# New instruction lists and PSUM banks for an attention block with cached keys and values

## The chip, the cores and the metric

The kernel runs on one core of a Trainium2 chip. The metric is the device time of one execution in microseconds (us), as the median of several runs. A profile of one execution shows where its time goes.

## The reference

```python
B, Sq, D = 8, 112, 640
H, Sk, Dh = 32, 512, 192
def reference(x, k_cache, v_cache, wq, wo):
    q = (x @ wq).reshape(B, Sq, H, Dh).transpose(0, 2, 1, 3)
    scores = jnp.einsum("bhqd,bhkd->bhqk", q, k_cache) * (Dh ** -0.5)
    p = softmax(scores, axis=-1)
    o = jnp.einsum("bhqk,bhkd->bhqd", p, v_cache)
    return o.transpose(0, 2, 1, 3).reshape(B, Sq, H * Dh) @ wo
```

All inputs are bf16. There is no mask; the keys and values are as long for every query.

## The kernel before

The 32 heads are worked in four rounds of 8 heads, and a round goes through the 8 batches. One batch of one round has its 8 heads in two halves, so there are 64 *steps* n = 0 to 63, each with four heads. Two *groups* g of four batches share a round, g = 0 to 7.

The program is a set of named operations. Each has an engine, the operations that it depends on, and an `emit` function that issues its instructions:

- ('XT', c) transposes a piece of x on TensorE (PE), and ('evX', c) copies it from PSUM to SBUF.
- ('Q', g, lp, c) is five matmuls of 448 columns that make 128 rows of the queries of a group (line 720 of the profile), and ('evQ', g, lp, c) copies them to `qr` as bf16 (line 146 on ScalarE (ACT), line 147 on VectorE (DVE)). ('qc', n) copies halves of them to `qh` (lines 761 and 762).
- ('KN', i, ...) loads plain keys of the first seven batches, ('KT', i, p) transposes a pair of heads of them with 24 small matmuls (line 672), and ('evK', i, p, t) copies the halves to `kt`. The keys of later batches, ('K', i), are transposed by DMA as they are loaded.
- ('Sm', n, j) and ('St', n, j) are the scores of a step: four matmuls each, the first on the whole array, the second on two halves of its rows at once (line 773).
- ('smax', n, i) scales one head's scores out of PSUM and takes its extreme (DVE, line 830), ('exp', n, i) is the exponential (ACT, line 835), ('rc', n, j) the reciprocal of the sums (DVE, line 847), ('norm', n, i) the scaling of the probabilities (DVE, line 839).
- ('PT', n) transposes the probabilities with 32 small matmuls (line 874), and ('evPT', n, 0) and ('evPT', n, 1) copy the narrow (768 columns) and the wide part (1024) to `pT_sb`. For five late steps a DMA does it, ('TD', n).
- ('PVt', n) and ('PVm', n, j) multiply by the values, the first on halves of the array's columns (line 906), the second on the whole array (line 918); ('evPV', n) copies the result to `oT_sb` (ACT).
- ('O', g, m, part) multiplies by wo (line 940), ('oacc', g, m) adds up over rounds in `accT` (DVE). ('O6', ...), ('OL', ...) and ('oaccL', ...) are the same for the last two batches, ('OF', b) transposes the result back, ('oout', b) copies it out of PSUM, ('OUT', b) stores it.
- ('V', i, half), ('WQ', r, lp, n) and ('WO', r, half) are loads of values and weights.

An engine does its operations strictly in the order of a list that stands in the program as a table: `ORDER_PE`, `ORDER_ACT`, `ORDER_DVE` and `ORDER_SP` (the queue on SyncE that issues all DMAs). `BANKS` gives the PSUM bank of every result that PE makes. Waits follow from the dependencies, and two rules add more: whoever writes a bank waits until its previous contents were copied out, and a load waits until the load some 1.5 MB ahead of it in `ORDER_SP` has landed:

```python
AHEAD = 0.95
for i, op in enumerate(ORDER_SP):
    behind = [k for k in range(i) if sum(map(size, ORDER_SP[k + 1:i])) >= AHEAD]
    if behind and op[0] != "OUT":
        P.ops[op]["deps"] = P.ops[op]["deps"] + [ORDER_SP[behind[-1]]]
for op in ORDER_PE:
    for bank, evacs in tiles(op):
        P.ops[op]["banks"] = P.ops[op]["banks"] + holder.get(bank, [])
        holder[bank] = evacs
```

An operation's list also decides its engine. A copy out of PSUM runs on ACT or DVE, whichever list holds it:

```python
def copy(name, e, dst, src):
    if P.ops[name]["eng"] == "ACT":
        return e.activation(dst, src, ACTF.Copy)
    return e.tensor_copy(dst, src)
```

A load of keys or values reuses one of four or three buffers, so it also waits for the step that last read it; a load of wq waits for the Q matmuls of the round before.

Of the kernel before, what the change touches and what calls it, by code (L numbers as in the profile page):

```python
# [52 lines left out]
def build_mha_kernel(nc, x, k_cache, v_cache, wq, wo, out):  # L53
# [33 lines left out]
    with ExitStack() as es:  # L87
# [145 lines left out]
        def pv_all(n):  # L233
# [11 lines left out]
            ('PVm', 0, 0), ('PVm', 0, 1), ('PVt', 1), ('PVm', 1, 0), ('PVm', 1, 1), ('KT', 3, 3), ('Sm', 4, 0),  # L245
# [17 lines left out]
            ('Sm', 15, 0), ('Sm', 15, 1), ('St', 15, 0), ('St', 15, 1), ('PT', 13), ('PVt', 12), ('PVm', 12, 0),
            ('PVm', 12, 1), ('PVt', 13), ('PVm', 13, 0), ('PVm', 13, 1), ('Sm', 16, 0), ('Sm', 16, 1), ('St', 16, 0),
            ('St', 16, 1), ('PT', 14), ('Q', 3, 0, 1), ('Q', 3, 2, 0), ('Q', 3, 1, 0), ('Sm', 17, 0), ('Sm', 17, 1),
            ('St', 17, 0), ('St', 17, 1), ('PT', 15), ('PVt', 14), ('PVm', 14, 0), ('PVm', 14, 1), ('PVt', 15),
# [20 lines left out]
            ('Sm', 31, 1), ('St', 31, 0), ('St', 31, 1), ('PT', 29), ('O', 2, 4, 1), ('PVt', 28), ('PVt', 29),
            ('PVm', 29, 0), ('PVm', 29, 1), ('PVm', 28, 0), ('PVm', 28, 1), ('Sm', 32, 0), ('Sm', 32, 1), ('St', 32, 0),
            ('St', 32, 1), ('PT', 30), ('O', 2, 3, 0), ('Q', 5, 0, 0), ('O', 2, 3, 1), ('Q', 5, 2, 0), ('Sm', 33, 0),
            ('Sm', 33, 1), ('St', 33, 0), ('St', 33, 1), ('PT', 31), ('Q', 5, 3, 2), ('Q', 5, 1, 0), ('Sm', 34, 0),  # L290
            ('Sm', 34, 1), ('St', 34, 0), ('St', 34, 1), ('PVt', 30), ('PVt', 31), ('PVm', 30, 0), ('PVm', 30, 1),
# [910 lines left out]
```

## Time and profile before

| what | value |
|---|---|
| median of 3 runs | 439.31 us (437.9 to 439.82) |
| the profiled execution | 438.76 us, span of its instructions 437.0 us |
| PE busy | 423.3 us, 97% of the span |
| DVE busy | 363.1 us, 83% |
| ACT busy | 343.7 us, 79% |
| matmuls, weight loads | 6805 each |
| moved by DMA | 122.04 MB, 279 GB/s |

The span runs from the first to the last instruction; the run's time has 1.76 us around it. In the rows that follow, a line such as L720 is a line of the program, "x5" counts instructions, and a wait stands in brackets with what ended it; "issue" means that the profile shows nothing that the engine waited for.

### The profile page before, as it was taken

How to read it: one execution, taken by the hardware profiler on the slowest of the kernel's cores; microseconds unless marked ns; L12 is line 12 of the kernel's file. 1: busy time of each engine (PE TensorE's matmuls, PEld its weight loads, DVE VectorE, ACT ScalarE, POOL GpSimd, SP SyncE). 2: the span in 40 equal slices, each digit the busy share in tenths (PEclk: the TensorE clock that was granted, in tenths of full speed). 3: DMA queues.
4: the chain of work that ended last, by engine and by line, in shares of the span. 5: the costliest groups of instructions: out<-in, count | busy, mean ns of one | idle time of the engine just before them, and what ended most of it. 6: DMA issues, size and time to landing. Idle time of an engine off the chain costs nothing.

```text
span 437.0 us, 16234 instructions
## 1 busy us (share of the span) xinstructions
PE 423.3 (97%) x6805; PEld 290.2 (66%) x6805; DVE 363.1 (83%) x1169; ACT 343.7 (79%) x770; POOL 0.7 (0%) x6
## 2 busy tenths in 40 slices
PE   7999979999999999999999999999999999999996
PEld 4666756667677566666667666666766666576896
DVE  1479987989699889898999887889799878999872
ACT  2699979998579787988878777887878856985774
POOL 0000000000000000000000000000000000000000
PEclk9999999999999999999999999999999999999999
DMA  7998999999999999999999999999999999999972
GB/s 255 366 354 289 331 358 287 213 289 342 238 288 286 283 256 257 362 263 255 308 240 237 337 255 256 364 352 287 232 242 376 204 247 349 289 252 252 239 201 82
DMA packets 222858, 122.04 MB, mean 279 GB/s; under 512 B 165312, under 2 KB 222784, under 8 KB 222784
## 3 DMA queue, kind: packets, MB, share of 16 engines
q1 hardware_dynamic: 222784, 120.99, 106.6%
q8 instruction: 54, 0.88, 0.8%
q14 instruction: 20, 0.16, 0.1%
HBM read 78.22 MB, written 1.15 MB: 182 GB/s over the span
## 4 chain that ended last, share of the span: by engine, by line
PE 85%; DVE 7%; ACT 4%; DMA 2%; issue 1%; SPq 0%; DVEq 0%; ACTq 0%
PE ps L940 19%; PE ps L720 19%; PE ps L773 18%; PE ps L918 12%; PE ps L906 7%; PE ps L874 5%; DVE s_sb L830 4%; PE ps L672 2%; ACT p_sb L835 2%; DMA wq_sb<-in_wq_dram 2%; DVE p_sb L839 1%; ACT kt L146 1%; PE ps L973 1%; ACT qr L146 1%; DVE pT_sb L147 1%
## 5 line engine op out<-in xcount | busy, mean ns | idle before, releaser
L835 ACT ACTIVATE p_sb<-s_sb,nmx 112x512 bf16<-112x512 f32 x256 | 183.0, 718 | 32.8 <-DVE s_sb L830 25.6
L830 DVE TENSOR_SCALAR_CACHE_REDUCE s_sb<-ps 112x512 f32<-112x512 f32 x256 | 169.2, 683 | 23.3 <-PE ps L773 19.1
L720 PE MATMUL ps<-xT_sb,wq_sb 128*128 128x448 bf16 x480 | 103.2, 356 | 3.1 <-DMA wq_sb<-in_wq_dram 2.1
L773 PE MATMUL ps<-kt,qr 128*128 128x256 bf16 (+1 forms) x512 | 95.6, 273 | 1.1 <-ACT oT_sb L146 0.4
L940 PE MATMUL ps<-oT_sb,wo_sb 128*128 128x448 bf16 (+1 forms) x480 | 93.3, 341 | 0.3 <-DVE pT_sb L147 0.2
L773 PE MATMUL ps<-kt,qh 128*128 128x256 bf16 (+1 forms) x512 | 87.5, 272 | 0.0
L839 DVE TENSOR_SCALAR p_sb<-p_sb,rinv 112x512 bf16<-112x512 bf16 x256 | 81.2, 346 | 1.5
L720 PEld LDWEIGHTS ps<-xT_sb,wq_sb 128*128 128x128 bf16 x480 | 43.1, 98 | 41.9 <-DMA wq_sb<-in_wq_dram 2.8
L940 PEld LDWEIGHTS ps<-oT_sb,wo_sb 128*128 128x128 bf16 x480 | 44.3, 98 | 35.4 <-DVE pT_sb L147 0.8
L146 ACT ACTIVATE oT_sb<-ps 128x672 bf16<-128x672 f32 x64 | 46.1, 725 | 22.3 <-PE ps L918 21.7
L773 PEld LDWEIGHTS ps<-kt,qr 128*128 128x128 bf16 (+1 forms) x512 | 44.3, 96 | 25.7 <-issue 14.3
L146 ACT ACTIVATE qr<-ps 128x448 bf16<-128x448 f32 x96 | 49.7, 541 | 12.8 <-PE ps L720 12.1
L146 ACT ACTIVATE pT_sb<-ps 128x768 bf16<-128x768 bf16 x59 | 47.0, 800 | 10.3 <-PE ps L874 10.2
L918 PE MATMUL ps<-pT_sb,vt 128*128 128x112 bf16 x944 | 54.9, 213 | 0.0
L918 PEld LDWEIGHTS ps<-pT_sb,vt 128*128 128x128 bf16 x944 | 47.4, 98 | 4.1
L835 ACT ACTIVATION_READ_ACCUMULATOR p_sb<-s_sb,nmx 112x1 f32 x256 | 49.7, 194 | 0.0
L773 PEld LDWEIGHTS ps<-kt,qh 128*128 128x128 bf16 (+1 forms) x512 | 43.9, 96 | 6.1
L147 DVE COPY pT_sb<-ps 128x1024 bf16<-128x1024 bf16 x59 | 40.2, 682 | 2.4 <-PE ps L874 1.3
L874 PE MATMUL ps<-ident,p_sb 64*128 64x64 bf16 (+1 forms) x1888 | 37.4, 186 | 0.9 <-DVE p_sb L839 0.5
L874 PEld LDWEIGHTS ps<-ident,p_sb 64*128 64x128 bf16 (+1 forms) x1888 | 33.2, 94 | 6.9 <-DVE p_sb L839 2.6
L906 PE MATMUL ps<-pT_sb,vt 128*64 128x112 bf16 x944 | 32.8, 215 | 1.4 <-DVE s_sb L830 0.5
L906 PEld LDWEIGHTS ps<-pT_sb,vt 128*64 128x64 bf16 x944 | 25.5, 110 | 12.2 <-issue 3.4
(53 smaller groups left out, 228.2 us busy)
## 6 DMA issues: line engine op xcount, KB each, us to landing
vt<-in_v_cache_dram SPq DMA_DIRECT2D x64, 768.0 KB, 6.7
wo_sb<-in_wo_dram SPq DMA_DIRECT2D x8, 960.0 KB, 8.2
wq_sb<-in_wq_dram SPq DMA_DIRECT2D x14, 480.0 KB, 5.7
wo_sb<-in_k_cache_dram SPq DMA_DIRECT2D x6, 768.0 KB, 7.1
accT<-in_k_cache_dram SPq DMA_DIRECT2D x6, 768.0 KB, 7.2
vt<-in_k_cache_dram SPq DMA_DIRECT2D x2, 768.0 KB, 8.5
out_dram<-xT_sb SPq DMA_DIRECT2D x8, 140.0 KB, 2.5
wq_sb<-in_wq_dram SPq DMA_DIRECT2D x1, 960.0 KB, 7.5
```

What stands on the lines that cost most here:

```text
L146: return e.activation(dst, src, ACTF.Copy)
L147: return e.tensor_copy(dst, src)
L672: ends = [e.transpose(psb[:, bank + t, y * 64:(y + 1) * 64], kn[i][64 * t:64 * t + 64, 2 * p + u, c * 128:(c + 1) * 128], ident[64 * t:64 ...
L720: mm = e.matmul(ps[:, bank, 0:SG], w, v, start=(dc == 0), stop=(dc == DC - 1))
L773: return e.matmul(ps[:, 2 * j + odd, hs], q, ktb[j][lo:hi, :, blk, h * 128:(h + 1) * 128], start=first, stop=last, skip_group_check=True)
L830: return e.tensor_scalar(s_sb[:, a, :].rearrange("p (e c) -> p e c", e=2), ps[0:SQ, 2 * j:2 * j + 2, h * 256:(h + 1) * 256], -scale, None, ...
L835: return e.activation(p_sb[:, k, :], s_sb[:, a, :], ACTF.Exp, bias=nmx[:, k:k + 1], scale=-1.0, accum_out=rsum[:, k:k + 1])
L839: return e.tensor_scalar(p_sb[:, k, :], p_sb[:, k, :], rinv[:, k:k + 1], None, op0=ALU.mult)
L874: ends.append(e.transpose(psb[:, bank + t, i * w:(i + 1) * w], p_sb[lo:hi, (4 * n + k) % 8, q * 128:(q + 1) * 128], ident[lo:hi, lo:hi]))
L906: mm = e.matmul(ps[64 * h:64 * h + 64, b0 + j, SQ:2 * SQ], vtb[:, h0 + 2 * j + h, d0:d0 + 64], pT(j, h, q), start=(q == 0), stop=(q == 3))
L918: mm = e.matmul(ps[:, b0 + j, 2 * h * SQ:(2 * h + 1) * SQ], vtb[:, h0 + 2 * j + h, d0:d0 + 128], pT(j, h, q), start=(q == 0), stop=(q == 3))
L940: mm = e.matmul(ps[:, bank_of["O", g, m], 0:nc_], wo_sb[:, k, m * 128:(m + 1) * 128], oT_sb[:, g % 2, k, 0:nc_], start=(k == 0), stop=(k = ...
```

## The change

`ORDER_PE`, `ORDER_ACT`, `ORDER_DVE`, `ORDER_SP` and `BANKS` are replaced by others. The new tables were searched offline in two steps, first with a K or V load as one piece, and then with its halves as pieces of their own. The operations, their instructions, the dependencies, the buffers and the two rules above are the same; a line fewer in the tables moves all later lines up by one. 80 copies out of PSUM go from ACT to DVE and 43 from DVE to ACT.

```diff
         ORDER_PE = [
...
-            ('Sm', 6, 0), ('Sm', 6, 1), ('St', 6, 0), ('St', 6, 1), ('KT', 4, 1),
-            ('KT', 4, 2), ('KT', 4, 0), ('KT', 4, 3), ('Q', 2, 1, 0), ('PT', 4),
...
+            ('PVm', 3, 1), ('Sm', 7, 0), ('Sm', 7, 1), ('KT', 4, 1),
+            ('KT', 4, 2), ('St', 7, 0), ('St', 7, 1), ('KT', 5, 1), ('Q', 2, 1, 0), ('PT', 5),
...
         BANKS = [
-            (('XT', 0), 1), (('XT', 1), 4), (('XT', 3), 2), (('XT', 2), 3), (('Q', 0, 1, 1), 1),
+            (('XT', 0), 5), (('XT', 1), 4), (('XT', 3), 4), (('XT', 2), 7), (('Q', 0, 1, 1), 5),
```

On PE, before: the values of step 2, the scores of step 6 (L773, whole and split), the four transposes of the keys of batch 4, and five Q matmuls.

```order
L918 MATMUL ps<-pT_sb,vt 128x112 x16
L773 MATMUL ps<-kt,qr 128x256
L773 MATMUL ps<-kt,qh 128x256 x2
L773 MATMUL ps<-kt,qr 128x256 x2
L773 MATMUL ps<-kt,qh 128x256 x2
L773 MATMUL ps<-kt,qr 128x256 x2
L773 MATMUL ps<-kt,qh 128x256 x2
L773 MATMUL ps<-kt,qr 128x256 x2
L773 MATMUL ps<-kt,qh 128x256 x2
L773 MATMUL ps<-kt,qr 128x256
L672 MATMUL ps<-ident,accT 128x64 x96
L720 MATMUL ps<-xT_sb,wq_sb 128x448 x5
```

Now, around step 7, where two of these transposes stand:

```order
L772 MATMUL ps<-kt,qr 128x256
L772 MATMUL ps<-kt,qh 128x256 x2
L772 MATMUL ps<-kt,qr 128x256 x2
L772 MATMUL ps<-kt,qh 128x256 x2
L772 MATMUL ps<-kt,qr 128x256
L671 MATMUL ps<-ident,accT 128x64 x48
L772 MATMUL ps<-kt,qr 128x256
L772 MATMUL ps<-kt,qh 128x256 x2
L772 MATMUL ps<-kt,qr 128x256 x2
L772 MATMUL ps<-kt,qh 128x256 x2
L772 MATMUL ps<-kt,qr 128x256
L671 MATMUL ps<-ident,wo_sb 128x64 x24
```

The transposes, which use halves of the array's rows, moved between the whole (first five rows) and the split scores (the five after them) of a step; 15 of the 64 steps now have something between the two.

On DVE, the first copies before (xT_sb is x, kt the keys, qr and qh the queries; L830 is smax):

```order
L147 COPY xT_sb<-ps 128x5x128 x2
L147 COPY kt<-ps 128x6x2x64 x3
L147 COPY xT_sb<-ps 128x5x128
L147 COPY kt<-ps 128x6x2x64
L761 COPY qh<-qr 64x2x336
L762 COPY qh<-qr 64x2x336
L830 TENSOR_SCALAR s_sb,nmx<-ps 112x512 x4
```

and now:

```order
L147 COPY xT_sb<-ps 128x5x128 x3
L147 CAST qr<-ps 128x448
L147 COPY xT_sb<-ps 128x5x128
L760 COPY qh<-qr 64x2x336
L761 COPY qh<-qr 64x2x336
L147 COPY kt<-ps 128x6x2x64
L147 CAST qr<-ps 128x448 x3
L147 COPY kt<-ps 128x6x2x64 x3
```

The copies of Q from f32 to bf16 (CAST) came to DVE, 35 of 96 in all; before, ACT had all of them.

On SP, from the first loads of values (vt) before (wq_sb<-in_wq_dram is a load of wq, wo_sb and accT <-in_k_cache_dram are plain keys):

```order
L167 DMA vt<-in_v_cache_dram 128x4x768 x4
L205 DMA wq_sb<-in_wq_dram 128x5x384
L189 DMA wo_sb<-in_k_cache_dram 128x4x768 x2
L189 DMA accT<-in_k_cache_dram 128x4x768 x2
L167 DMA vt<-in_v_cache_dram 128x4x768 x4
```

and now:

```order
L167 DMA vt<-in_v_cache_dram 128x4x768 x5
L189 DMA wo_sb<-in_k_cache_dram 128x4x768 x2
L167 DMA vt<-in_v_cache_dram 128x4x768
L189 DMA accT<-in_k_cache_dram 128x4x768
L205 DMA wq_sb<-in_wq_dram 128x5x384
L189 DMA accT<-in_k_cache_dram 128x4x768
```

The load of wq moved behind five others, and halves of one load no longer stand side by side. At the end of the list, ('V', 31, 0) and ('V', 31, 1) moved ahead of the first two stores of the output.

More of the change, by code (lines that the diff above doesn't have):

```diff
@@ L237, in build_mha_kernel @@
             ('XT', 0), ('XT', 1), ('XT', 3), ('XT', 2), ('Q', 0, 1, 1), ('Q', 0, 0, 0), ('Q', 0, 0, 1), ('Q', 0, 1, 0),
[7 rows of a table removed]
-            ('PVm', 0, 0), ('PVm', 0, 1), ('PVt', 1), ('PVm', 1, 0), ('PVm', 1, 1), ('KT', 3, 3), ('Sm', 4, 0),
[11 rows of a table removed]
-            ('St', 11, 1), ('PVt', 8), ('PVt', 9), ('PVm', 9, 0), ('PVm', 9, 1), ('PVm', 8, 0), ('PVm', 8, 1),
[3 rows of a table removed]
-            ('PVt', 10), ('O', 0, 3, 0), ('PVm', 10, 0), ('PVm', 10, 1), ('O', 0, 1, 1), ('PVt', 11), ('PT', 12),
-            ('PVm', 11, 0), ('PVm', 11, 1), ('O', 0, 2, 0), ('O', 0, 2, 1), ('Q', 3, 0, 0), ('O', 0, 3, 1), ('Q', 3, 0, 2),
@@ L263, in build_mha_kernel @@
[L263 to L266, printed above, removed]
[19 rows of a table removed]
-            ('PVm', 27, 0), ('PVm', 27, 1), ('PVm', 26, 0), ('PVm', 26, 1), ('PT', 28), ('O', 2, 4, 0), ('Sm', 31, 0),
@@ L287, in build_mha_kernel @@
[L287 to L291, printed above, removed]
@@ L292, in build_mha_kernel @@
-            ('PVm', 31, 0), ('PVm', 31, 1), ('PT', 32), ('Q', 5, 0, 1), ('O', 3, 0, 0), ('O', 3, 0, 1), ('Sm', 35, 0),
-            ('Sm', 35, 1), ('St', 35, 0), ('St', 35, 1), ('PT', 33), ('O', 3, 3, 0), ('O', 3, 3, 1), ('PVt', 32),
-            ('PVt', 33), ('PVm', 32, 0), ('PVm', 32, 1), ('Q', 5, 0, 2), ('PVm', 33, 0), ('PVm', 33, 1), ('Sm', 36, 0),
-            ('Sm', 36, 1), ('St', 36, 0), ('St', 36, 1), ('PT', 34), ('O', 3, 1, 0), ('O', 3, 1, 1), ('Q', 5, 1, 2),
-            ('Sm', 37, 0), ('Sm', 37, 1), ('St', 37, 0), ('St', 37, 1), ('PT', 35), ('O', 3, 2, 0), ('O', 3, 2, 1),
@@ L297, in build_mha_kernel @@
-            ('Q', 5, 1, 1), ('PVt', 35), ('PVt', 34), ('PVm', 34, 0), ('PVm', 34, 1), ('PVm', 35, 0), ('PVm', 35, 1),
[5 rows of a table removed]
-            ('Q', 6, 2, 0), ('PVt', 38), ('PVm', 38, 0), ('PVm', 38, 1), ('PVt', 39), ('Q', 6, 3, 0), ('PVm', 39, 0),
[3 rows of a table removed]
[17 rows of a table added]
+            ('PVm', 6, 1), ('Q', 2, 3, 0), ('PT', 8), ('KT', 6, 3), ('PVt', 7), ('PVm', 7, 0), ('PVm', 7, 1),
+            ('Q', 2, 3, 2), ('Q', 2, 1, 2), ('Q', 2, 2, 0), ('KT', 6, 1), ('PT', 9), ('Q', 2, 3, 1), ('Sm', 11, 0),
+            ('Sm', 11, 1), ('St', 11, 0), ('St', 11, 1), ('PVt', 9), ('PVt', 8), ('PVm', 9, 0), ('PVm', 9, 1),
[5 rows of a table added]
@@ new lines, in build_mha_kernel @@
+            ('St', 15, 0), ('St', 15, 1), ('PT', 13), ('PVt', 12), ('PVm', 12, 0), ('PVm', 12, 1), ('PVt', 13),
+            ('PVm', 13, 0), ('PVm', 13, 1), ('Sm', 16, 0), ('Sm', 16, 1), ('St', 16, 0), ('St', 16, 1), ('PT', 14),
+            ('Q', 3, 0, 2), ('Q', 3, 0, 1), ('Q', 3, 1, 0), ('Q', 3, 0, 0), ('Sm', 17, 0), ('Sm', 17, 1), ('Q', 3, 2, 0),
+            ('PT', 15), ('St', 17, 0), ('St', 17, 1), ('PVt', 14), ('PVt', 15), ('PVm', 14, 0), ('PVm', 14, 1),
[3 rows of a table added]
+            ('PVt', 16), ('PVm', 16, 0), ('PVm', 16, 1), ('PVm', 17, 0), ('PVm', 17, 1), ('Sm', 20, 0), ('Sm', 20, 1),
[5 rows of a table added]
@@ new lines, in build_mha_kernel @@
+            ('PVm', 21, 0), ('PVm', 21, 1), ('PVm', 20, 0), ('PVm', 20, 1), ('Q', 4, 0, 1), ('Sm', 24, 0), ('Sm', 24, 1),
+            ('St', 24, 0), ('St', 24, 1), ('PT', 22), ('Q', 4, 1, 0), ('Q', 4, 2, 1), ('Q', 4, 0, 0), ('Sm', 25, 0),
+            ('Sm', 25, 1), ('St', 25, 0), ('St', 25, 1), ('PT', 23), ('Q', 4, 1, 1), ('Q', 4, 1, 2), ('Q', 4, 0, 2),
+            ('Sm', 26, 0), ('Sm', 26, 1), ('PVt', 22), ('PVt', 23), ('PVm', 23, 0), ('PVm', 23, 1), ('PVm', 22, 0),
[3 rows of a table added]
+            ('PVt', 24), ('PVm', 24, 0), ('PVm', 24, 1), ('Q', 4, 2, 2), ('PVt', 25), ('PVm', 25, 0), ('PVm', 25, 1),
[4 rows of a table added]
@@ new lines, in build_mha_kernel @@
+            ('PVt', 29), ('PVm', 29, 0), ('PVm', 29, 1), ('PVm', 28, 0), ('PVm', 28, 1), ('Sm', 32, 0), ('Sm', 32, 1),
[5 rows of a table added]
+            ('Sm', 36, 1), ('PVt', 33), ('PVt', 32), ('PVm', 32, 0), ('PVm', 32, 1), ('PVm', 33, 0), ('PVm', 33, 1),
+            ('St', 36, 0), ('St', 36, 1), ('PT', 34), ('O', 3, 2, 0), ('Q', 5, 2, 1), ('Sm', 37, 0), ('Sm', 37, 1),
+            ('St', 37, 0), ('St', 37, 1), ('PT', 35), ('Q', 5, 2, 2), ('O', 3, 2, 1), ('PVt', 35), ('PVt', 34),
+            ('PVm', 35, 0), ('PVm', 35, 1), ('O', 3, 1, 0), ('PVm', 34, 0), ('PVm', 34, 1), ('Sm', 38, 0), ('Sm', 38, 1),
[5 rows of a table added]
@@ L307, in build_mha_kernel @@
+            ('Q', 6, 1, 0), ('PVt', 38), ('PVt', 39), ('PVm', 39, 0), ('PVm', 39, 1), ('PVm', 38, 0), ('PVm', 38, 1),
[3 rows of a table added]
             ('St', 44, 0), ('St', 44, 1), ('PT', 42), ('PVt', 40), ('PVm', 40, 0), ('PVm', 40, 1), ('Q', 6, 2, 1),
@@ L309, in build_mha_kernel @@
             ('PT', 43), ('O', 4, 3, 0), ('O', 4, 3, 1), ('PVt', 42), ('PVm', 42, 0), ('PVm', 42, 1), ('Sm', 46, 0),
[6 rows of a table removed]
-            ('PT', 48), ('PVt', 46), ('PVm', 46, 0), ('PVm', 46, 1), ('PVt', 47), ('PVm', 47, 0), ('PVm', 47, 1),
-            ('O', 5, 1, 0), ('O', 5, 0, 0), ('Sm', 51, 0), ('Sm', 51, 1), ('St', 51, 0), ('St', 51, 1), ('PT', 49),
-            ('O', 5, 1, 1), ('O', 5, 0, 1), ('Q', 7, 2, 0), ('Sm', 52, 0), ('Sm', 52, 1), ('St', 52, 0), ('St', 52, 1),
-            ('PVt', 49), ('PVt', 48), ('PVm', 48, 0), ('PVm', 48, 1), ('PVm', 49, 0), ('PVm', 49, 1), ('Q', 7, 2, 2),
[5 rows of a table removed]
[12 rows of a table added]
@@ L557, in build_mha_kernel @@
             ('KN', 0, 4, 4), ('KN', 1, 0, 4), ('KN', 1, 4, 4), ('KN', 2, 0, 4), ('KN', 2, 4, 4), ('V', 2, 0), ('V', 2, 1),
[16 rows of a table removed]
-            ('OUT', 1), ('OUT', 2), ('OUT', 4), ('OUT', 6), ('OUT', 7)]
-        BANKS = [
[54 rows of a table removed]
[16 rows of a table added]
+            ('OUT', 4), ('OUT', 3), ('OUT', 6), ('OUT', 7)]
+        BANKS = [
[55 rows of a table added]
         for kind, *a in ORDER_SP:
```

421 lines of the change are left out of this document (210 added, 211 removed), and 290 rows, old and new, of tables (BANKS, ORDER_PE, ORDER_SP).

## The prediction

> **What bounds the kernel now.** I read the page first, then the busy time by stage, then the instructions in order of time at single places. The page:
>
> ```profile
> span 437.0 us, 16234 instructions
> PE 423.3 (97%) x6805; PEld 290.2 (66%) x6805; DVE 363.1 (83%) x1169; ACT 343.7 (79%) x770; POOL 0.7 (0%) x6
> PE   7999979999999999999999999999999999999996
> DMA  7998999999999999999999999999999999999972
> q1 hardware_dynamic: 222784, 120.99, 106.6%
> q8 instruction: 54, 0.88, 0.8%
> ```
>
> PE is busy in all but 13.7 us, and the change keeps every matmul, so what a new order can win is those 13.7 us and whatever of the 423.3 us is cost of order. The second row to note is DMA: its queue is full from the first slice to the last but one. The stages:
>
> ```profile
> core 0: us, PE busy (x) PEld busy (x) DVE busy (x) ACT busy (x) POOL busy (x), PEclk, DMA share, GB/s
> 0.00:10.00 10.00, 6.77 (x45) 4.68 (x46) 1.83 (x8) 2.79 (x4) 0.70 (x6) 1.00 0.76 245
> 36.00:60.00 24.00, 22.17 (x473) 15.76 (x471) 22.96 (x75) 23.28 (x53) 0.00 (x0) 1.00 0.99 329
> 60.00:70.00 10.00, 7.58 (x150) 4.79 (x151) 7.15 (x21) 6.93 (x13) 0.00 (x0) 0.83 1.07 366
> 70.00:108.00 38.00, 36.99 (x722) 25.37 (x722) 34.82 (x113) 36.86 (x84) 0.00 (x0) 1.00 1.05 270
> 108.00:185.00 77.00, 77.00 (x1153) 51.64 (x1151) 66.36 (x212) 58.08 (x134) 0.00 (x0) 1.00 1.17 282
> 185.00:400.00 215.00, 213.41 (x3265) 143.50 (x3262) 190.61 (x621) 171.97 (x395) 0.00 (x0) 1.00 1.15 278
> 424.00:437.00 13.00, 9.41 (x237) 8.82 (x234) 3.88 (x12) 5.56 (x8) 0.00 (x0) 0.95 0.23 69
> ```
>
> Three regimes. The ends (3.23 us of PE idle before 10 us, 3.59 after 424) wait for the first loads and the last output. From 36 to 108 us, steps 2 to 13, the K and Q copies pile up: DVE is busy for 22.96 and ACT for 23.28 of 24 us, and ACT for 36.86 of 38 from 70 to 108. There PE's order is not the limit, the two copying engines are. From 108 to 400 us PE is the limit: 1.59 us idle in 292. The hole is at 60 to 70, where all three engines rest:
>
> ```profile
> 60.28 0.74 PE L672 MATMUL ps<-ident,accT 64*128 64x64 bf16 x37 [0.31 <-ACT kt L146]
> 62.79 0.35 PE L672 MATMUL ps<-ident,accT 64*128 64x64 bf16 x11 [1.77 <-issue]
> 63.07 1.54 PE L720 MATMUL ps<-xT_sb,wq_sb 128*128 128x448 bf16 x5
> ```
>
> ```profile
> PE ps L672 <- issue: 1.8, 1, 1.8
> PE ps L720 <- DMA wq_sb<-in_wq_dram: 2.1, 2, 1.8
> ```
>
> The last fence is from the view of waits: who waited for whom, total, times, longest. The wait of 1.77 us falls inside one operation, 11 matmuls before the end of ('KT', 4, 3), whose semaphores were met at its first matmul; so no list entry releases it. The instruction queue's row fits: 54 loads of 0.88 MB are 16 KB each, and 6805 matmuls with 6805 weight loads are 252 PE instructions for each. I take it that PE had run through its instructions faster than the full DMA queue brought the next block. After it the granted clock is 0.83 over ten microseconds. DVE and ACT, 96 and 97% busy from 36 to 60 us, drop to 7.15 and 6.93 of 10: about 2.9 us of the stage that the copies bound were lost.
>
> **The change, part by part.** *Matmul order.* What a switch between whole-array matmuls and split ones (half the rows or columns) costs shows in starts:
>
> ```profile
> 148.51 0.27 PE L773 MATMUL ps<-kt,qr 64*128 64x256 bf16 x1
> 148.62 0.63 PE L874 MATMUL ps<-ident,p_sb 64*128 64x64 bf16 x32
> 149.18 1.12 PE L720 MATMUL ps<-xT_sb,wq_sb 128*128 128x448 bf16 x5
> 150.13 2.43 PE L940 MATMUL ps<-oT_sb,wo_sb 128*128 128x448 bf16 x12
> ...
> 153.71 0.27 PE L773 MATMUL ps<-kt,qr 64*128 64x256 bf16 x1
> 153.93 0.98 PE L906 MATMUL ps<-pT_sb,vt 128*64 128x112 bf16 x32
> 154.84 1.75 PE L918 MATMUL ps<-pT_sb,vt 128*128 128x112 bf16 x32
> 156.42 1.11 PE L720 MATMUL ps<-xT_sb,wq_sb 128*128 128x448 bf16 x5
> 157.46 0.64 PE L874 MATMUL ps<-ident,p_sb 64*128 64x64 bf16 x32
> ```
>
> Five Q matmuls take 0.95 us up to another whole-array group (149.18 to 150.13) and 1.04 up to split transposes (156.42 to 157.46): 0.09. From the last score matmul it is 0.11 us to transposes with the same split and 0.22 to values split by columns: 0.11. So a switch costs 0.10 us. Counted in the two lists, before has 254 switches and after 240, because transposes now stand between the whole and the split scores of a step. Of the 14, 6 lie in steps 2 to 11, where copies bound the stage and they win nothing; 8 lie in the PE-bound part: 8 x 0.10 = **-0.8 us**. The other order of the tail lets the last sums (oaccL) start one group of matmuls earlier; that group is 12 of the 60 matmuls of 112 columns, and what waited for the sum was
>
> ```profile
> 433.14 0.49 PE L1022 MATMUL ps<-ident,accT 128*112 128x128 bf16 x5 [0.22 <-DVE accT L1006]
> ```
>
> so **-0.2 us** at most, which I take. The first loads stay as they are up to the sixteenth, so the 3.23 us of the start stay.
>
> *Copies change engine.* 35 of the 96 Q copies go to DVE, 26 of the wide pT halves to ACT, 24 narrow ones to DVE. Their prices:
>
> ```profile
> L146 ACT ACTIVATE qr<-ps 128x448 bf16<-128x448 f32 x96 | 49.7, 541 | 12.8 <-PE ps L720 12.1
> L146 ACT ACTIVATE pT_sb<-ps 128x768 bf16<-128x768 bf16 x59 | 47.0, 800 | 10.3 <-PE ps L874 10.2
> L147 DVE COPY pT_sb<-ps 128x1024 bf16<-128x1024 bf16 x59 | 40.2, 682 | 2.4 <-PE ps L874 1.3
> L147 DVE COPY kt<-ps 128x768 bf16<-128x768 bf16 x31 | 16.5, 551 | 11.4 <-PE ps L672 11.3
> L954 DVE COPY accT<-ps 128x448 f32<-128x448 f32 x10 | 6.2, 618 | 0.3 <-PE ps L940 0.3
> ```
>
> A Q copy on DVE has no row. The bounds are 551 x 448/768 = 321 ns, if it ran like the bf16 copy of kt, and 618 ns, the f32 copy of the same 448 columns. I take 618: same width and same source type. The Trainium skill (VectorE: DVE Perf Modes, Why PSUM operands drop a tier) says that a PSUM operand in fp32 holds VectorE to its lowest rate; that speaks for the upper bound and against this part of the change, and the rows agree (448 columns of f32 in 618 ns, 1024 of bf16 in 682). Over the whole kernel DVE gains 35 x 0.618 + 24 x 0.551 - 26 x 0.682 = +17.1 us, to 380 of 437, and ACT loses 35 x 0.541 = 18.9 and 24 x 0.800 = 19.2 and gains 26 wide halves, by columns 26 x 0.800 x 1024/768 = 27.7: -10.4 us. From 185 to 400 us DVE is busy for 190.61/215 = 89%; with 17.1/437 = 4% more it has 93%: no cost by itself. Between steps 2 and 13, by the lists, DVE has 4 kt and 6 Q copies and 3 narrow halves more and 4 wide halves less: 2.2 + 3.7 + 1.7 - 2.7 = +4.9 us, and ACT 4 kt, 4 Q and 2 narrow halves less and 4 wide more: 3.3 + 2.2 + 1.6 - 4.3 = -2.8 us. In its three rows above the two together have 64.9 + 67.1 = 132 of 144 us, and get 134. That is the same limit with the load on the other engine, so I forecast that this stage repeats its time, its one hole included: **0**, with bounds below.
>
> *Load order.* Before, a wq load stands in SP's queue where it must wait for Q matmuls, and everything behind it waits too:
>
> ```profile
> 22.09 7.38 SPq L167 DMA_DIRECT2D vt<-in_v_cache_dram  x4
> 33.08 0.37 SPq L205 DMA_DIRECT2D wq_sb<-in_wq_dram  x1
> ```
>
> After, that load stands five loads later. The stream of loads then runs ahead by at most the 33.08 - 29.47 = 3.6 us without an issue; but the only load that PE waits for in the view of waits is wq, twice, both within the idle time before 10 us, so this buys slack and no time: 0. At the end the last two V loads no longer stand behind two outputs; the same holds.
>
> **Sum.** The profiled execution took 438.76 us (span 437.0 and 1.76 around it), and the median of the three runs is 439.31, 0.55 more. -0.8 - 0.2 = -1.0 gives 437.8 against the profiled execution and **438.3** as a median.
>
> **The rivals.**
>
> *The hole does not come back.* It hangs on where the blocks of instructions fall among dense matmuls, and the new list moves that. The 2.9 us go, and the time is 435.4. For it: only one such wait of over 1 us in 54 blocks (the row of the view of waits). Against it is the next rival's count. The Trainium skill (Runtime: NRT & Kernel Launch, Instruction fetch mechanics) says that PE streams its instructions in 16 KiB blocks and that crossing a block is mostly hidden. By that rule density would cost nothing and this rival would be the likeliest; the row with 1.77 us and no releaser speaks against it.
>
> *More holes (slower).* Small matmuls use up instructions fastest: 32 transposes in 0.56 us (148.62 to 149.18) against 5 Q matmuls in 0.95. Priced by such pitches, the blocks of 128 matmuls around steps 5 to 9 last 6.1, 3.7, 6.1 and 4.8 us before; the hole is at the end of the 3.7. After, four in a row last 3.8, 4.2, 4.9 and 4.0 us. If two more of them wait, the stage loses 2 x 2.9 = 5.8 us: 444.1. It decides as soon as two blocks wait beyond the one that did. Against it: before has two more blocks of 4.8 and 4.9 us, by the same pitches, around steps 2 and 4, and no hole there; and each such wait gives the next block time.
>
> *DVE becomes the bound of steps 2 to 13.* It would be busy 64.9 + 4.9 = 69.8 of 72 us, 97%. If it can be kept only as busy as ACT was, 67.1/72 = 93%, the stage lasts 69.8/0.93 = 75.1: +3.1 us, and with the -1.0, 441.4. For it: smax and norm of every step queue behind the copies. Against it: ACT ran at 97% from 36 to 60 us.
>
> *The change does not act:* if switches were hidden elsewhere, 439.3, within the forecast's range.
>
> **How the numbers follow.** The forecast gets 0.40; since 0.5% (2.2 us) is about what a measurement of this kernel can tell from no change, that is 0.08 faster, 0.30 same, 0.02 slower. The hole that goes: 0.24, all faster. More holes: 0.18 (0.01 same, 0.17 slower). DVE as the bound: 0.18, at 441.4 on the border of 441.5, so 0.06 same and 0.12 slower. Sums: faster 0.32, same 0.37, slower 0.31. The range reaches from 434.5 (the hole gone, 435.4, less 0.9, half of the 1.9 us by which the three runs before differ) to 444.0 (more holes); the forecast's own is 436.5 to 440.5.
>
> **What would show it.** In the profile after: PE busy lower by about 1 us between 108 and 400 us; DVE about 380 us and ACT about 333 in all; a CAST of qr on DVE near 618 ns; the number and length of PE waits put down to "issue" between 36 and 108 us, and the granted clock there; DVE's busy share in that stage. A load named as what PE waits for after 10 us, or a stage from 108 to 400 us that is longer than now, would make the working wrong.

## The result, and the profile after

| | before | after |
|---|---|---|
| median of 11 runs each | 438.65 us (436.19 to 440.33) | 441.72 us (440.06 to 446.74) |
| ratio, with its 95% interval | | 1.007 (1.0041 to 1.0099) |
| the profiled execution, its span | 438.76 us, 437.0 | 440.45 us, 438.5 |

The kernel became slower by 0.7%, 3.1 us; the forecast was 438.3 us, 1.0 us less than the median then known. The ratios in this document leave out executions more than 1.5% above the quickest of the same kernel, here one of the eleven (446.74 us). The profiled execution shows 1.5 us of the loss in its span; it is one of the quicker ones. The page of the changed kernel, busy time and DMA:

```profile
span 438.5 us, 16237 instructions
PE 423.1 (96%) x6805; PEld 290.2 (66%) x6805; DVE 378.2 (86%) x1206; ACT 333.7 (76%) x733; POOL 0.7 (0%) x6
DMA  8999999999999999999999999999999999999972
q1 hardware_dynamic: 222784, 120.99, 107.5%
q8 instruction: 54, 0.88, 0.8%
```

PE's busy time is the old one less 0.2 us. The span grew because PE is idle for 15.4 us instead of 13.7. The stages, busy time of each engine:

```profile
core 0: us, PE busy (x) PEld busy (x) DVE busy (x) ACT busy (x) POOL busy (x), PEclk, DMA share, GB/s
0.00:10.00 10.00, 7.35 (x47) 5.14 (x48) 2.22 (x9) 2.59 (x4) 0.70 (x6) 1.00 0.81 260
36.00:60.00 24.00, 22.22 (x504) 15.71 (x498) 23.77 (x78) 23.39 (x52) 0.00 (x0) 1.00 1.03 341
60.00:70.00 10.00, 9.27 (x200) 6.46 (x201) 9.85 (x32) 9.51 (x20) 0.00 (x0) 1.00 0.99 316
70.00:108.00 38.00, 35.68 (x661) 24.27 (x661) 33.24 (x103) 28.23 (x63) 0.00 (x0) 0.96 1.11 275
108.00:185.00 77.00, 76.36 (x1180) 51.69 (x1173) 70.71 (x228) 58.80 (x131) 0.00 (x0) 1.00 1.14 286
185.00:400.00 215.00, 212.04 (x3220) 142.06 (x3218) 194.14 (x625) 167.12 (x374) 0.00 (x0) 1.00 1.15 273
424.00:438.00 14.00, 10.88 (x254) 10.24 (x245) 3.67 (x10) 6.14 (x10) 0.00 (x0) 1.00 0.23 71
```

From 36 to 108 us PE is idle for 4.8 us where it was 5.3. Step 13 begins at 106.4 us (106.7 before) and step 14, with other work of PE in between, at 113.2 (112.1), so that stage repeated its time to within about 1 us. From 108 to 400 us the idle time is 3.6 us where it was 1.6. Three of PE's waits, in order of time, from the instructions on PE (start, us, operation, in square brackets the wait ahead and its releaser): the hole inside ('KT', 5, 3), the second values matmul of step 51, that of step 59:

```profile
71.25 0.42 PE L671 MATMUL ps<-ident,wo_sb 64*128 64x64 bf16 x14
73.78 0.30 PE L671 MATMUL ps<-ident,wo_sb 64*128 64x64 bf16 x9 [2.12 <-issue]
...
365.57 0.58 PE L905 MATMUL ps<-pT_sb,vt 128*64 128x112 bf16 x16 [1.41 <-DMA vt<-in_v_cache_dram]
...
408.71 0.58 PE L905 MATMUL ps<-wq_sb,vt 128*64 128x112 bf16 x16 [0.59 <-DMA wq_sb<-p_sb]
```

A hole is there again, nine matmuls before the end of another operation, with a lower clock behind it (0.96 over 38 us). The other two waits are new: PE waits for the load V(25, 1) and for TD(59). A load as PE's wait after 10 us is what the prediction named as the sign that its working is wrong.

Price every operation on PE by the shortest time from its start to the next one's in the trace of before. That gives some 406 us for the old list and 1.3 to 1.5 us less for the new one, an estimate that depends a little on how the operations are grouped: the 14 switches fewer, 0.1 us each, are there. Beyond its price the new run lost some 2.9 us more than the old. Of these, 1.6 are at V(25, 1) and 0.8 at TD(59); the start has 0.4 less, and the remaining 0.8 or so are scattered over short waits.

The reason for V(25, 1) can be read from SP's queue. After:

```profile
317.03 5.40 SPq L167 DMA_DIRECT2D vt<-in_v_cache_dram  x4
325.31 14.91 SPq L158 DMA_TRANSPOSE kt<-in_k_cache_dram  x2
...
340.32 16.55 SPq L158 DMA_TRANSPOSE kt<-in_k_cache_dram  x2
356.92 5.89 SPq L167 DMA_DIRECT2D vt<-in_v_cache_dram  x4
```

and before:

```profile
317.19 7.01 SPq L158 DMA_TRANSPOSE kt<-in_k_cache_dram  x1
324.29 10.84 SPq L167 DMA_DIRECT2D vt<-in_v_cache_dram  x6
336.88 22.01 SPq L158 DMA_TRANSPOSE kt<-in_k_cache_dram  x3
```

Before, V(25) stood third of three pairs behind K(26), and three K loads came after it: it landed at 341.0 us for a use at 366.5, 25 us early. After, the first two pairs stand ahead of K(26), and the second load of the first pair waits 2.9 us for its buffer with nothing behind it let through; then come four K loads, 7.4 to 9.0 us from one issue to the next, and only then V(25). It lands at 365.4 us, 0.1 us before its matmul starts.

The second such load is WQ(3, 0), which PE needs at 278.1 us before and at 278.0 after. It landed at 272.9 us before and at 277.0 after. Before, it stood ahead of two V loads, and after, behind them (the row at 267.93). Before:

```profile
268.04 1.15 SPq L205 DMA_DIRECT2D wq_sb<-in_wq_dram  x2
269.23 2.77 SPq L167 DMA_DIRECT2D vt<-in_v_cache_dram  x2
```

and after:

```profile
267.93 1.08 SPq L167 DMA_DIRECT2D vt<-in_v_cache_dram  x2
271.43 2.33 SPq L205 DMA_DIRECT2D wq_sb<-in_wq_dram  x3
```

The margin, the time from a load's landing to its first use, shrank from 5.3 to 1.0 us. In this execution that cost nothing. The next runs show what it costs in others.

### The profile page after: what moved, and what is told of

It reads as the page before. It is cut to its first block, busy times and chain, and to the rows that moved or that the text cites. A ratio compares the mean times of both kernels' runs of the same rounds, so it can differ in the third digit from the quotient of the medians.

```text
span 438.5 us, 16237 instructions
## 1 busy us (share of the span) xinstructions
PE 423.1 (96%) x6805; PEld 290.2 (66%) x6805; DVE 378.2 (86%) x1206; ACT 333.7 (76%) x733; POOL 0.7 (0%) x6
## 4 chain that ended last, share of the span: by engine, by line
PE 71%; DVE 16%; ACT 5%; DMA 4%; issue 3%; SPq 0%; DVEq 0%; ACTq 0%
PE ps L772 16%; PE ps L719 15%; PE ps L939 13%; PE ps L917 10%; DVE s_sb L829 7%; PE ps L905 6%; PE ps L873 5%; ACT p_sb L834 3%; DVE p_sb L838 3%; DMA wq_sb<-p_sb 2%; PE ps L671 2%; DMA vt<-in_v_cache_dram 2%; DVE pT_sb L147 1%; ACT pT_sb L146 1%; DVE qr L147 1%
## 5 line engine op out<-in xcount | busy, mean ns | idle before, releaser
L719 PE MATMUL ps<-xT_sb,wq_sb 128*128 128x448 bf16 x480 | 101.7, 354 | 1.3 <-ACT xT_sb L146 0.9
L772 PE MATMUL ps<-kt,qr 128*128 128x256 bf16 (+1 forms) x512 | 96.8, 273 | 1.7 <-DVE s_sb L829 1.2
L146 ACT ACTIVATE pT_sb<-ps 128x768 bf16<-128x768 bf16 (+1 forms) x61 | 53.9, 891 | 10.4 <-PE ps L873 10.3
L146 ACT ACTIVATE qr<-ps 128x448 bf16<-128x448 f32 x61 | 32.0, 538 | 15.0 <-PE ps L719 14.9
L147 DVE COPY pT_sb<-ps 128x1024 bf16<-128x1024 bf16 (+1 forms) x57 | 35.4, 626 | 5.1 <-PE ps L873 5.0
```

The source lines that it names most:

```text
L719: mm = e.matmul(ps[:, bank, 0:SG], w, v, start=(dc == 0), stop=(dc == DC - 1))
L772: return e.matmul(ps[:, 2 * j + odd, hs], q, ktb[j][lo:hi, :, blk, h * 128:(h + 1) * 128], start=first, stop=last, skip_group_check=True)
```

## The experiments

They ran in five groups, each on one chip beside the kernel before. A ratio is to the kernel before on that chip.

### The kernel again, and one load moved

No edit in the first (e1). In the second (e2):

```diff
-            ... ('K', 28), ('K', 29), ('V', 25, 0), ('V', 25, 1), ('V', 26, 0), ...
+            ... ('K', 28), ('V', 25, 0), ('V', 25, 1), ('K', 29), ('V', 26, 0), ...
```

> The changed kernel once more, unaltered, to see which waits of its first profile come back. If the waits belong to the lists, the wait of a split values matmul for V(25, 1) near 365 us (1.41 us) and the one for TD(59) near 408 us (0.59 us) come back within 0.5 us, and the hole of about 2 us inside ('KT', 5, 3) at 72 to 74 us comes back at the same instruction; ratio 1.007. If they are chance, other operations wait and the time scatters by more than 2 us.

> V(25, 0) and V(25, 1) issued ahead of K(29) instead of behind it, nothing else. Theory that the load order costs: they land some 7 us earlier, the wait of 1.41 us near 365 us is gone, K(29) lands about 4 us later with some 20 us to spare, and the time falls by 1.4 us to a ratio of about 1.004. Rival, that the copies on DVE set the pace there: the wait moves to another operation within the next steps and the ratio stays at 1.007.

e1: 446.95 us, ratio 1.015 (1.0104 to 1.0196), on this chip twice the loss. The hole and the wait for V(25, 1) came back at the same instructions. The one for TD(59) did not (it landed 0.5 us early), and a longer wait is new. The view of waits of PE in e1:

```profile
PE ps L719 <- DMA wq_sb<-in_wq_dram: 3.5, 1, 3.5
PE ps L671 <- issue: 2.7, 1, 2.7
PE ps L772 <- DVE s_sb L829: 1.8, 2, 1.2
PE ps L905 <- DMA vt<-in_v_cache_dram: 1.5, 1, 1.5
```

The first row is WQ(3, 0): it landed at 282.5 us, 5.5 us later than in the first profile, and the margin was gone. Against the first profile e1 lost 7.2 us, 5.4 of them between steps 38 and 43, where this wait lies.

e2: 445.85 us, 1.0145 (1.0104 to 1.0187). The wait at V(25, 1) is gone (landed 7.1 us early; steps 54 to 57 lose 1.7 us less), as expected, and the time did not fall: WQ(3, 0) was as late as in e1 (283.6 us), and 0.9 us came back after step 62. The move does what it should, and it does not decide.

### Where the blocks of instructions fall

```diff
-                mm = e.matmul(ps[:, 5, 0:256], zeros[:, 0:128], zeros, start=True, stop=True)
+                mm = e.matmul(ps[:, 5, 0:160], zeros[:, 0:128], zeros[:, 0:160], start=True, stop=True)
...
-            idle(e, 18)
+            idle(e, 28)
```

e4 is the same in the kernel before, with 92 matmuls of 40 columns.

> 28 warm-up matmuls of 160 columns instead of 18 of 256, in time in which PE waits for the first loads anyway: every later instruction of PE stands 20 places further on in its blocks of 256. Between 28 and 108 us the shortest block then lasts 5.4 us instead of 4.5. Theory, that the hole is a block of instructions that arrives late: the hole at 72 to 74 us (2.1 us, then low clock) is gone, and the time falls by 2 to 3 us to a ratio of 1.001. Rival, that the hole belongs to ('KT', 5, 3) or to the DMA state at that time: it stays and the ratio is 1.007.

> The kernel before with 92 warm-up matmuls of 40 columns instead of 18 of 256: its instructions stand 148 places further on in their blocks, and the shortest block between 28 and 108 us lasts 5.3 us instead of 3.7 to 4.7. Theory, a late block: the hole at 61 to 63 us is gone, DVE and ACT stay busy over 90% from 60 to 70 us, and the time falls by the 2.9 us that I priced the hole at, ratio 0.993. Rival, that the hole only shifts time that the copies need anyway: it is gone and the ratio is 0.998 to 1.000.

e3: 447.98 us, 1.0186 (1.014 to 1.0231). e4: 443.18 us, 1.0106 (1.0058 to 1.0154). Both expectations failed: neither gained, and the kernel before lost 1%. PE's waits put down to "issue" in e3:

```profile
72.76 0.45 PE L671 MATMUL ps<-ident,wo_sb 64*128 64x64 bf16 x19 [1.14 <-issue]
81.06 0.80 PE L671 MATMUL ps<-ident,accT 64*128 64x64 bf16 x23 [2.09 <-issue]
```

and in e4:

```profile
59.60 0.70 PE L672 MATMUL ps<-ident,accT 64*128 64x64 bf16 x36 [1.46 <-issue]
71.99 0.65 PE L918 MATMUL ps<-pT_sb,vt 128*128 128x112 bf16 x10 [1.70 <-issue]
...
390.24 0.29 PE L773 MATMUL ps<-kt,qr 64*128 64x256 bf16 x2 [1.36 <-issue]
```

The holes moved with the blocks: the hole in ('KT', 5, 3) now starts ten matmuls earlier (x9 became x19, the 10 warm-ups added), and e4 has one in the scores of a step near 390 us, where there are no dense transposes. Counted over PE's matmuls, weight loads and semaphore instructions, the waits of over 1 us that are put down to "issue" stand at numbers such as 961, 1985, 2497, 2753, 3265 and 12481, all 193 more than a multiple of 256 to within two places, in every kernel. So they belong to blocks of 256 instructions, as I took it.

What I had wrong is that short blocks make them. The blocks ahead of e4's three stalls lasted 5.4 to 5.8 us and the one ahead of the hole of before, at 62.79 us, 4.9, which I had priced at 3.7. What adds to it is when the next block is fetched: in these stalls, in all profiles, its transfer on the instruction queue starts 2.7 to 6.7 us after the first instruction of the block ahead, takes 0.9 to 1.6 us, and PE goes on 1.2 to 1.6 us later. Which block is caught is not a matter of the lists alone either. The kernel before, unaltered (e5, below), has its one stall of over 1 us in ('PT', 2):

```profile
49.15 0.29 PE L874 MATMUL ps<-ident,p_sb 48*128 48x48 bf16 x9 [1.18 <-issue]
```

so a single profile does not show what a moved hole costs. e4 loses its 1% elsewhere: in its profile step 38 begins at 263.5 us (263.3 in e5) and step 63 at 421.0 (416.5). What makes a fetch start late was not found.

### Work taken away from PE

```diff
+                w_ = SQ if g == 1 else nc_
...
-                    mm = e.matmul(ps[:, bank_of["O", g, m], 0:nc_], wo_sb[:, k, m * 128:(m + 1) * 128],
-                                  oT_sb[:, g % 2, k, 0:nc_], start=(k == 0), stop=(k == KB - 1))
+                    mm = e.matmul(ps[:, bank_of["O", g, m], 0:w_], wo_sb[:, k, m * 128:(m + 1) * 128],
+                                  oT_sb[:, g % 2, k, 0:w_], start=(k == 0), stop=(k == KB - 1))
```

> The kernel before once more, to lay its loads beside those of the runs that follow. Theory that the stream of loads sets the pace from 100 us on in both kernels: the DMA queue q1 has under 6 us without a packet between 10 and 420 us, as in its first profile (3.8 us), and WQ(3, 0) lands 3 us or more before its Q matmul needs it. Rival, that PE sets it: every load from 100 to 400 us lands over 5 us early.

> The changed kernel with a part of the work left out: the 60 matmuls of ('O', 1, m, part) take 112 columns instead of 448, so PE has some 8 us less to do between 136 and 190 us; instructions, loads and copies are as many as before. If PE sets the pace from 108 to 400 us, the time falls by about 8 us, to a ratio of 0.99 to 1.0. If the loads do, PE waits for WQ(2, ...), WQ(3, ...) and V loads instead and the time falls by 1 to 3 us at most.

> The kernel before with the same part left out, 8 us of PE work in group 1 of the output matmuls. If PE sets the pace, the ratio is 0.982. If the loads do, it gains what slack they have, WQ(3, 0) 3.5 to 5.3 us, WQ(3, 3) 0.3 and V(19, 1) 1.3 us in the first profile: 1 to 3 us, ratio 0.993 to 0.998.

e5, a single execution, took 438.35 us. Its load queue had 3.5 us without a packet between 10 and 420 us, and WQ(3, 0) landed 5.0 us early, both much as in the profile of before and as the theory of the loads had it; WQ(3, 3) landed 0.4 us early, so not every load has the 5 us of the rival. e8: 439.01 us, 0.9964 (0.9927 to 1.0002); e7: 446.03 us, 1.0173 (1.0117 to 1.0228), four executions. Neither gained what it had less to do. In e7 PE waits 3.6 us for WQ(3, 0) and 2.7 for V(25, 1). In e8 the reason is not the one I expected. The stretch in question, in e5 and in e8:

```profile
136.00:190.00 54.00, 54.00 (x812) 36.19 (x809) 47.35 (x156) 43.86 (x103) 0.00 (x0) 1.00 1.12 300
136.00:190.00 54.00, 48.82 (x817) 34.35 (x817) 47.57 (x156) 44.18 (x103) 0.00 (x0) 0.97 1.11 302
```

and the longest of the waits of PE there in e8 (total, times, longest):

```profile
PE ps L773 <- DVE s_sb L830: 2.6, 4, 1.3
```

In e5 PE is busy all the time there. With less to do it is idle for 5.2 us; for half of that it waits for the scaling of the scores on DVE, and for most of the rest for the copies of the transposed probabilities (1.2 us on ACT, 0.6 on DVE). Step 26 begins at 186.8 us in e8 and at 187.0 in e5. No load is late there. So PE, busy all the time, did not set the pace of these steps alone. The chain from the scores over DVE and ACT to the transposes is what it waited for instead; DVE is busy for 88% there, so its work alone does not fill the time either.

### Loads moved, and load orders exchanged

e6 takes e2's move, and V(20) out of the way of WQ(3, 0):

```diff
-            ... ('K', 22), ('V', 20, 0), ('V', 20, 1), ('WQ', 3, 0, 1), ... ('WO', 2, 1), ('V', 21, 0), ...
+            ... ('K', 22), ('WQ', 3, 0, 1), ... ('WO', 2, 1), ('V', 20, 0), ('V', 20, 1), ('V', 21, 0), ...
```

e9 is the changed kernel with the whole `ORDER_SP` of before, e10 the kernel before with that of the changed one.

> The changed kernel with two moves in the load order: V(20, 0) and V(20, 1) behind WO(2, 1) instead of ahead of WQ(3, 0), so that the loads from WQ(3, 0) to WO(2, 1) land some 4 us earlier, and V(25, 0), V(25, 1) ahead of K(29). V(20) keeps some 20 us. Theory of the loads: the wait of 3 to 5 us at Q(6, 0, 1) near 280 us and the 1.4 us at PVt 51 are gone and the time falls by 4 to 5 us against the changed kernel of the first experiment, to a ratio of about 1.004. Rival, that the copies on DVE or the blocks of instructions make the difference: the ratio stays at 1.012 to 1.015.

> The changed kernel with the load order (the SP list) of the kernel before; PE, ACT, DVE and banks as changed. So far K(30) and K(31), the last of a set of loads that is the same in both, had landed at 395 to 399 us in four profiles of the kernel before and its variants and at 397 to 405 us in six of the changed one, with the queue almost never empty in either. Theory that the new load order makes the stream slower: K(31) lands by 397 us and the ratio is 1.000 within 0.004. Rival, that what the other engines do slows the transfers: K(31) lands at 400 us or later and the ratio stays at 1.012 or more.

> The mirror: the kernel before with the load order of the changed one. Theory of the load order: K(31) lands at 400 us or later and the ratio is 1.008 to 1.015. Rival, the engine lists: K(31) lands by 397 us and the ratio is within 0.003 of 1.000.

e6: 446.42 us (440.73 to 451.85), 1.0132 (1.0095 to 1.0168): not to be told from e1, so the ratio is the rival's, though no run shows the copies or the blocks to be the reason. Both waits are gone in its profile (WQ(3, 0) 1.7 us early, V(25, 1) 2.2), and step 58 begins at 383.7 us against 391.5 in e1. Then steps 60 to 61 take 12.8 us where the first profile has 4.0. The row on ACT in that profile (an execution of 448.2 us, the third longest of eleven):

```profile
404.23 0.72 ACT L834 ACTIVATE p_sb<-s_sb,nmx 112x512 bf16<-112x512 f32 x1 [7.34 <-DMA wq_sb<-p_sb]
```

An exponential waits for TD(57) to empty its buffer. TD(57) stands behind K(30) and K(31), which landed by 401.9 us, 6.6 us later than in e5 and e8 (395.2 and 395.3). What the two moves won, the end of the same stream took back in this execution.

e10: 1.0083 (1.0036 to 1.013), resting on two executions of 441.2 and 444.1 us; the other seven took 448.1 to 454.8, and its profile is of one of 448.1. All nine are longer than any of the kernel before beside them (437.1 to 440.6). The load order alone thus brings the kernel before to the time of the changed one or beyond, with K(31) at 403.0 us as its theory had it, and with the wait for WQ(3, 0) (the longest of the three):

```profile
PE ps L720 <- DMA wq_sb<-in_wq_dram: 5.5, 3, 3.7
```

e9: 455.14 us, 1.0371 (1.0337 to 1.0405), where I had forecast 1.000; K(31) landed at 400.8 us, as the rival had it. So it is not that the new order is slow and the old one quick: the new lists with the old order are late too. Of the 13.0 us by which the span of e9 exceeds that of the first changed profile, 4.5 are there when step 63 begins (1.9 of them when step 0 begins), and 8.5 follow. The longest wait behind it:

```profile
436.00 0.96 PE L905 MATMUL ps<-pT_sb,vt 128*64 128x112 bf16 x16 [5.07 <-DMA vt<-in_v_cache_dram]
```

In the old order V(31) stands behind OUT(3) and OUT(0), and the new PE list makes output 3 late: OUT(3) was issued at 428.2 us, and at 415.3 in the kernel before. The order of loads and the lists of the engines are one table; halves of two such tables cost more than either.

### Q copies, and the depth of the queue

e11 puts 24 of the 35 Q copies back on ACT; e12, e13 and e14 change one number:

```diff
-    AHEAD = 0.95
+    AHEAD = 1.45
```

> The changed kernel with 24 of the 35 Q copies that went to DVE (those of groups 3 to 7) back on ACT, each where it started in time. DVE has some 13 to 15 us less. If DVE's load sets the pace after 108 us, the time falls by 1.5 us or more (ratio 1.009 or less). If the loads do, nothing moves beyond 1 us (1.010 to 1.015).

> The changed kernel with AHEAD = 1.45 instead of 0.95, so that a load may be issued while some 0.75 MB more is under way. If the stream loses time because the queue runs low now and then, K(31) lands 3 us or more earlier (by 400 us) and the ratio falls below 1.009. If transfers themselves are the limit, K(31) does not land earlier, while blocks of PE instructions wait longer behind the fuller queue: two holes or more, ratio 1.015 or above.

> The changed kernel with AHEAD = 0.45 instead of 0.95: one load of V fewer is under way at a time. Deeper (1.45) was 451.7 us, holes of up to 2.7 us and K(31) at 407 us. Theory, that a fuller queue delays blocks of instructions and the other transfers alike: holes below 1 us, the time falls by 3 us or more, ratio 1.007 or less. Rival, that the queue then runs dry between loads: K(31) lands later than 405 us, ratio above 1.015.

> The kernel before with AHEAD = 0.45. By the same theory its hole at 61 us shrinks and the ratio is 0.993 to 0.998; by the rival the queue runs dry and it is 1.005 or more.

e11: 444.19 us, 1.0115 (1.0071 to 1.016), so no gain that can be told from e1 on its chip; its profile takes 0.7 us more than e1 from step 14 to step 38, where PE waits for no load. Nothing speaks for the copies on DVE as the cause. e12: 451.66 us, 1.0279 (1.024 to 1.0319); K(31) landed at 407 us, and the longest of PE's waits put down to "issue" were 2.5, 1.6 and 0.4 us. e13: 485.93 us, 1.1035 (1.0977 to 1.1092); e14: 487.52 us, 1.1065 (1.1003 to 1.1128). My theory for these two was wrong by some 45 us, and its rival had the direction right. The queue did not run dry as a whole, though: it was never without a packet between 10 and 420 us, but moved 255 GB/s over the span of e13 where the first changed profile has 278. PE's waits in e13:

```profile
PE ps L719 <- DMA wq_sb<-in_wq_dram: 16.7, 4, 11.3
PE ps L671 <- DMA wo_sb<-in_k_cache_dram: 9.1, 2, 7.4
```

One V load (0.75 MB) less under way, and the stream falls behind PE by up to 11 us at one load. In the changed kernel the depth of 0.95 sits between two losses; in the kernel before only the shallower one was run.

### Work taken out of the stream, and out of both

```diff
+                if i == 16:
+                    return e.dma_start_transpose(kt[:, i % KS].rearrange("p a m c -> p (a m) c")[:, 0:1, :], src[:, 0:128])
```

e17 and e18 have this edit and the narrow output matmuls. The load reads a sixth of its 1.5 MB (twice the 768 KB of a V load); the expectation of e15 has these megabytes half as large, but the time taken out, 5/6 of the 6.9 us of a K load, stands.

> The changed kernel with a part left out: K(16) transposes only one of its six pieces, 0.13 instead of 0.75 MB read, which takes some 5.7 us out of the stream of loads near 210 us; PE, ACT and DVE do all they did. If the stream sets the pace, the time falls by 4 to 6 us, ratio 1.000 to 1.004. If PE or the copies do, it does not fall (1.012).

> The kernel before with the same part left out. If its stream sets the pace too, the time falls by 2 to 6 us (ratio 0.987 to 0.995); if PE does, it stays within 1 us (0.998 to 1.000). The same kernel with 8 us less PE work had 0.996, with an interval that held 1.

> The kernel before with both parts left out: 8 us of PE work (group 1 of the output matmuls at 112 columns) and five sixths of the load K(16), 5.7 us of the stream. Each alone left the time where it was (0.996 and 1.000). Theory, that PE and the stream of loads are equally long and each covers a cut in the other: together they take 3 to 5 us off, ratio 0.988 to 0.993. Rival, that a third limit (the copies, or the chain of steps at the end) holds the time: 0.997 or more.

> The changed kernel with both parts left out. 8 us less PE work alone gave 1.017, the smaller load alone 1.005. By the theory of two equal paths the two together gain 3 to 5 us over the smaller load: ratio 0.993 to 0.998. By the rival: 1.004 or more.

| left out | before | after |
|---|---|---|
| nothing | 1 | 1.007 and 1.015 on two chips |
| 8 us of PE work | 0.9964 (0.9927 to 1.0002) | 1.0173 (1.0117 to 1.0228) |
| 5.7 us of the stream | 1.0002 (0.9971 to 1.0032) | 1.0048 (1.0012 to 1.0083) |
| both | 1.0005 (0.9976 to 1.0034) | 1.0052 (1.0021 to 1.0084) |

In the kernel before nothing shows, not even both, so the rival's ratio held. In e17's profile PE is idle for 4.8 us from 136 to 190 us as in e8, and the loads, 2.4 us earlier at K(22) than in e5, are back within 0.5 us at K(31): a load waits for its buffer, and so for the steps. But the two parts do not meet. PE's work is missing ahead of 171 us and the load from 190 us on; from 190 to 400 us PE is busy for 208.4 of 210 us in e17 as in e5 (208.1), so PE as the limit of these later steps is not excluded. In the changed kernel the smaller load brings WQ(3, 0) to a margin of 4.0 us (landed 274.4), no wait stands there, and the ratio is below e1's. But V(24, 1) now waits 6.4 us for its buffer, V(25, 1) lands 0.1 us early again, step 57 begins at 379.5 us (379.9 in the first profile), and the profile ends at 440.9, no earlier than the first.

## Why the prediction was wrong, point by point

The time moved by +3.1 us where -1.0 was forecast. That 441.7 us lies within the stated range is luck: its upper end came from the rival of more holes, and holes are not what the first profile lost its time to. That it is close to the 441.4 us of the rival of DVE is luck as well, as the stage of that rival did not grow by 3 us.

**The bound.** "From 108 to 400 us PE is the limit" was read from the busy row, and it failed where it was tested. PE was busy there for all but 1.6 us, but e8 took 8 us of work from it between 142 and 171 us and the steps went no faster. For the steps behind 190 us no run tests it; that PE, the softmax on DVE and ACT, and the loads are about equally long is a guess. From the bound followed that 0.8 us fewer on PE are 0.8 us of time. The switches did go (an estimate of 1.3 to 1.5 us for all 14), but PE's busy time fell by only 0.2 us in all. Between 108 and 400 us, where I had named 1 us, it fell by 2.0, and all of that became idle time.

**The load order: 0.** This is the step that failed most plainly, a term put at nothing. I argued from the view of waits that PE waits for no load after 10 us, so that a changed order "buys slack and no time". That view shows waits and not margins, and the order could also spend slack. It did: WQ(3, 0) from 5.3 to 1.0 us, V(25, 1) from 25 to 0.1, TD(59) from 0.9 to 0. In the first profile that cost 2.0 us of idle PE, where PE's idle time grew by 1.7; in e1 the wait for WQ(3, 0) cost 3.5. e10 shows the order by itself at 0.8%. It is the order as a whole: e2 and e6, which undo two of its parts, remove the waits and win no time. The shift of WQ(1, 0), to which I gave my sentence on loads, made no wait. V(31) ahead of the outputs kept its margin (3.0 us, 2.9 before), and e9 shows that its place was not free to choose: behind the outputs, the new lists wait 5.1 us for it.

**The stage from 36 to 108 us: 0, its one hole included.** Right to within about 1 us: one hole of 2.1 us where there was one of 1.8. That it was one again is partly luck: the kernel before has its stall elsewhere in e5 and none of over 1 us in e16, and the changed one has two in this stage in e3, e7, e9 and e18. The 2.9 us at which I priced it were too much: in e16, without it, step 14 begins at 111.2 us, 0.9 earlier than in the profile of before, and the span is 437.4, no shorter. That DVE could not go beyond 93% was the assumption of a rival, and it was wrong: DVE went to 23.77 of 24 us (99%). A wait of 1.2 us for DVE's scaling at step 6 is new, but PE's idle time in the stage did not grow. The Trainium skill (Runtime: NRT & Kernel Launch, Instruction fetch mechanics) has the crossing of a block mostly hidden; most of the 54 are, and in each profile up to three are not, at 1.1 to 2.7 us.

**The copies.** Right in the main: DVE 378.2 us (forecast 380), ACT 333.7 (333). The sums leave out the 3 copies of kt and the one of x that also go to DVE, net, and add up rows that overlap in part; that they hit so closely is partly luck. The price that had no row:

```profile
L147 DVE CAST qr<-ps 128x448 bf16<-128x448 f32 x35 | 21.4, 616 | 7.8 <-PE ps L719 7.8
```

It is 616 ns against the 618 taken; the Trainium skill (VectorE: DVE Perf Modes, Why PSUM operands drop a tier) agrees. e11 found no time in moving 24 of these copies back.

**The tail: -0.2.** Not there; the last sum is waited for as long as before:

```profile
434.61 0.49 PE L1021 MATMUL ps<-ident,accT 128*112 128x128 bf16 x5 [0.22 <-DVE accT L1005]
```

**Profile and median.** The forecast put 0.55 us between the profiled execution and the median; in the changed kernel it is 1.3 us: its executions scatter upwards (440 to 447 us). Used-up margins would do that; no run shows that they are the reason.

**What stays open.** The loss differs by chip (1.007, 1.015), which I could not vary by itself. The same set of loads up to K(22) had landed at 271.0 to 272.4 us in four profiles of the kernel before with its own load order, and at 271.4 to 277.0 us in nine with the new lists or the new load order, all at the depth of 0.95 and with no load cut. Some loads wait for buffers, such as V(24, 1); what else makes the stream slower was not found. That the scattered 0.8 us come from any one list is not shown, and the new `BANKS` were never run without the new lists.

## What to carry to other kernels

Before a reordering is priced, write down for each load its landing and its first use, in both orders, and price a used-up margin by how far the landing scatters between executions; a view of waits shows none of this. An engine that is busy all the time sets the pace only if taking work from it shortens the stage, so try that on the kernel before. A tuned table of matmuls, copies and loads has to be changed as one: half of it from another table cost 3.7% one way (e9) and 0.8% or more the other (e10).

## What the runs showed of the hardware that was not expected

- The depth of the load queue was worth more than any order run here: one V load (0.75 MB) less under way at a time cost 10% (486 and 488 us, e13 and e14), one more cost some 1 to 2% (e12).
- PE's instructions come in blocks of 256, and the block behind the running one can come late. In the stalls of over 1 us its transfer started 2.7 to 6.7 us after the first instruction of the block ahead and took 0.9 to 1.6 us. A block ahead that lasted 5.8 us did not hide it (e4, 390.24 us), and the same kernel has its stall at different blocks in different executions (62.79 us in the profile of before, 49.15 in e5).
- A landing is the slowest of 16 parts. In e1, between 275 and 300 us, most parts of a plain load ended within 0.6 us of the first, but the last came 1.9 us behind it for WQ(3, 0) and 3.5 for WQ(3, 3), and the lag went from load to load; the parts of the transposing load K(22) ahead of them had ended within 0.2 us.
